# Scores of the first eight attention jobs as one plain f32 product from the loaded q and k, in two alternating operand sets

## The chip, the cores and the metric

The kernel runs on one core of one Trainium2 chip. The metric is device time in microseconds (us), the median of three runs. Five engines work side by side, each in its own order: TensorE (PE; its weight loads are shown apart as PEld), VectorE (DVE), ScalarE (ACT), GpSimd (POOL) and SyncE (SP), which here only issues DMA transfers. ACT issues some too.

## The reference

Causal attention with a distance bias, then a two-layer feed-forward network (FFN). Batch 8, 8 heads, 576 positions, head width 64; the FFN goes from 512 to 2048 and back. q and k are drawn eight times wider than `_attn_setup` says.

```python
scores = scale * np.matmul(q, k.transpose(0, 1, 3, 2))        # scale = 1/8
cum = np.cumsum(np.maximum(s, 0.0), axis=-1)
bias = -(cum[:, :, :, None] - cum[:, :, None, :])
scores = np.where(causal, -1000000000.0, scores + np.minimum(bias, 0.0))
attn = softmax(scores)            # max taken off, exp, sum + 1e-9
x = attn @ v                      # (4608, 512) over all heads
h = x @ w_in
g = np.where(h >= 1, h, np.where(h <= -1, 0.0, (h + 1) ** 2 / 4))
out = g @ w_out
```

## The kernel before, in words

**Jobs.** Attention is cut into 64 jobs: a pair of heads `n` (four pairs to a batch) and a half `hf` of the query positions. Half 0 has 320 queries (query tiles 0 to 2), half 1 has 256 (tiles 3 and 4). The list `jobs` goes batch by batch, first the four pairs of half 0, then the four of half 1; the first eight jobs are all of batch 0. A job has six score units (`UNITS`): a query tile of one head against the keys up to it, 64, 192, 320, 448 or twice 288 keys wide. So a job of half 0 has 2 x (64 + 192 + 320) = 1152 score columns, one of half 1 has 2 x 448 + 4 x 288 = 2048.

**Scores from split operands.** `att_load` (L307) fetches q and k of a job as f32 into `rq` and `rk`, each twice, to partitions 0 to 63 and again to 64 to 127 (four transfers on SP's queue, L316). `att_prep` (L320) makes four operands in a rounded format (F32R) of them:

- `Q1`: upper half the rounded -q/8 (ACT, L325), lower half what the rounding lost (DVE, L336)
- `K1`: the rounded k in both halves (ACT, L334)
- `Q2`: the rounded -q/8 again (ACT, L335), with four more rows for the bias
- `K2`: what rounding k lost (GpSimd for the first twelve jobs, L339), with four bias rows

The bias rows are the running sums of s, as a high and a low part, fetched by transfers on ACT's queue (L329 and L330 from SBUF for the first two jobs, L332 and L333 from DRAM for the others). Each score unit is then two products into one PSUM tile `s` (two buffers): L384 (`Q1` by `K1`, 128 rows deep) and L385 (`Q2` by `K2`, 68 rows deep). There is one set of `Q1`, `K1`, `Q2`, `K2`, so the next job's operands can be made only when the last score unit of the job before has been multiplied.

**After the scores.** DVE adds the mask and keeps the row minimum (L390; the scores carry a minus sign, so the minimum belongs to the greatest score); ACT takes the exponential (L401); `weights_t` scales the weights and splits them into two f16 parts on POOL, ACT and DVE (L422 to L428), and SP transposes them by DMA (L429). `att_out` multiplies by v (L447).

**Stages.** In the first, the loop over `NPAIR` jobs (L574) decodes the 16 pieces of w_in, which lie in memory as 64-bit numbers (ACT L192 and L199, DVE L193 to L203), four pieces per job, beside the four jobs of half 0. The buffers of the pieces are few, so a piece is fetched when an earlier one is decoded. Then `w1.scale` (L585) finds one scale over all pieces: DVE reduces, PE transposes (tile `row_wi`), DVE shortens (`top_wi`), PE spreads (`col_wi`), DVE inverts (`r_wi`). Only then are the pieces split into f16 pairs and the FFN can start; w_out's pieces are fetched only after that scale, too. In the second stage w_out is decoded and split in the same way, beside jobs 4 to 7 of half 1 and the FFN products of half 0 (L502 the first layer, L541 the second). From then on each step has attention and FFN in a fixed mix.

**What sets the order.** The program is written as one stream; a scheduler orders each engine's instructions ahead of time by its own estimate of times and by priorities given in the code (`high_priority`, `issue_after`). On the chip every engine follows its list strictly.

Of the kernel before, what the change touches and what calls it, by code (L numbers as in the profile page):

```python
# [9 lines left out]
F32 = mybir.dt.float32  # L10
F32R = mybir.dt.float32r
# [3 lines left out]
AF = mybir.ActivationFunctionType  # L15
ALU = mybir.AluOpType
# [6 lines left out]
P = 128  # L23
# [8 lines left out]
BIG = 1e9  # L32
# [27 lines left out]
K_POOL = range(12)  # L60
V_POOL = 4
# [3 lines left out]
FIRST_N = 1  # L65
# [8 lines left out]
def attention_ffn(ctx: ExitStack, tc: tile.TileContext, qT, kT, vT, s, w_in, w_out, yT):  # L74
    nc = tc.nc
    LOADQ, CUMQ, FIRSTQ = nc.sync, nc.scalar, nc.sync
# [35 lines left out]
    def spread(dst, top, name):  # L112
# [11 lines left out]
        fill=BIG, base=448, channel_multiplier=1,  # L124
# [181 lines left out]
    def att_load(n, hf):  # L306
# [3 lines left out]
        W = q0 + N  # L310
        rq = ap.tile([P, 2, N], F32, tag="rq", bufs=1, name=f"rq{n}_{hf}")
        rk = ap.tile([P, 2, W], F32, tag="rk", bufs=1, name=f"rk{n}_{hf}")
        for t, src, c0 in ((rq, qT, q0), (rk, kT, 0)):
            sv = src[b, h0:h0 + 2, :, c0:W].rearrange("h d n -> d h n")
            for d0 in (0, D):
                (FIRSTQ if jobs.index((n, hf)) < FIRST_N else LOADQ).dma_start(t[d0:d0 + D], sv)  # L316
        raws[n, hf] = rq, rk

    def att_prep(n, hf):

        rq, rk = raws.pop((n, hf))
# [3 lines left out]
        A.activation(Q1[:, :, :N], rq, AF.Copy, scale=-0.125)  # L325
        if jobs.index((n, hf)) < CH_N:
            for hd in range(2):
                r = ch[2 * n + hd:2 * n + hd + 1]
                CUMQ.dma_start(Q2[D:D + 2, hd, :N].bitcast(F32), r[:, :, q0:W].bitcast(F32))  # L329
                CUMQ.dma_start(K2[D + 2:D + 4, hd, :W].bitcast(F32), r[:, :, :W].bitcast(F32))  # L330
        else:
            CUMQ.dma_start(Q2[D:D + 2, :, :N].bitcast(F32), cd[:, :, q0:W])  # L332
            CUMQ.dma_start(K2[D + 2:D + 4, :, :W].bitcast(F32), cd[:, :, :W])  # L333
        A.copy(K1[:, :, :W], rk)  # L334
        A.activation(Q2[:D, :, :N], rq[:D], AF.Copy, scale=-0.125)  # L335
        V.scalar_tensor_tensor(  # L336
            Q1[D:, :, :N], rq[D:], -0.125, Q1[D:, :, :N].bitcast(F32), ALU.mult, ALU.subtract
# [33 lines left out]
    def scores(n, i, hd, c0, c1):  # L371
# [12 lines left out]
        T.matmul(sc[:R, :c1 - c0], Q1[:, hd, qo:qo + R], K1[:, hd, c0:c1], start=True, stop=False)  # L384
        T.matmul(sc[:R, :c1 - c0], Q2[:KC, hd, qo:qo + R], K2[:KC, hd, c0:c1], start=False, stop=True)  # L385
# [278 lines left out]
```

## Time and profile before

| What | Value |
|---|---|
| Median of 3 runs | 1128.73 us (1127.24 to 1128.74) |
| Span of the profiled execution (first to last instruction) | 1126.2 us |
| The profiled execution's own time | not on the page; the median is 2.5 us over the span |
| PE busy | 988.1 us, 88% |
| DVE busy | 876.6 us, 78% |
| ACT busy | 745.2 us, 66% |
| POOL busy | 693.1 us, 62% |
| PE busy from 232 to 262 us | 29.88 of 30.00 us |
| PE busy from 30 to 60 us | 9.20 of 30.00 us |
| `r_wi` (scale of w_in) written | 88.2 us |

The page gives one execution. Busy shares are over the whole span and hide that the first fifth of the program is limited by other engines than the rest; the view by windows shows it. A row of the timeline has the start, the duration, the engine, the line and operation, output and inputs, and in brackets how long the engine had been idle and what released it. Durations of PE overlap, since matmuls are pipelined.

### The profile page before, as it was taken

The numbers are of one execution on the slowest core, as the hardware profiler recorded it, in microseconds if no ns is written. First come the engines' busy times: TensorE is split into PE (matmuls) and PEld (weight loads), VectorE is DVE, ScalarE is ACT, GpSimd is POOL, SyncE is SP. The second block draws the span as 40 slices with busy tenths as digits, with TensorE's granted clock in tenths as the row PEclk, the third lists the DMA queues.
The fourth block names the chain that finished last, engine by engine and source line by source line (L and its number), as shares of the span: only waits on it lengthen the run. The fifth ranks groups of instructions, "written<-read, shape, count | busy, mean of one in ns | idle before, by whom it ended". The sixth has DMA issues, their size and how long they took to land.

```text
span 1126.2 us, 25201 instructions
## 1 busy us (share of the span) xinstructions
PE 988.1 (88%) x8470; PEld 771.8 (69%) x8470; DVE 876.6 (78%) x2396; ACT 745.2 (66%) x1727; POOL 693.1 (62%) x1177
## 2 busy tenths in 40 slices
PE   1233587799999999989999999999999999899998
PEld 0122355578777877778777877787778777787787
DVE  7999996778777887778778877888788877787533
ACT  4667687677747775767657774777577765777432
POOL 3867279776547764676647754776467664765522
PEclk9997987889999999999999999999999999999999
DMA  8995546677739774778647763877467864666300
GB/s 235 214 204 149 164 110 137 123 158 163 151 74 190 153 172 86 150 170 144 142 86 189 165 143 75 191 169 166 86 148 171 152 136 84 157 156 138 66 24 20
DMA packets 343082, 158.05 MB, mean 140 GB/s; under 512 B 291112, under 2 KB 324264, under 8 KB 342952
## 3 DMA queue, kind: packets, MB, share of 16 engines
q1 hardware_dynamic: 333248, 146.50, 60.7%
q10 hardware_dynamic: 9704, 9.93, 2.8%
q8 instruction: 67, 1.10, 0.4%
q14 instruction: 63, 0.52, 0.1%
HBM read 75.33 MB, written 9.73 MB: 76 GB/s over the span
## 4 chain that ended last, share of the span: by engine, by line
PE 48%; DVE 6%; POOL 5%; issue 3%; ACT 3%; DMA 2%; ACTq 0%; DVEq 0%; POOLq 0%
PE h L502 20%; PE y L541 20%; PE px L447 3%; PE s L384 3%; PE s L385 2%; DMA pt<-pb 2%; DVE pb L428 1%; DVE Q L336 1%; POOL g L529 1%; POOL pb L422 1%; ACT u L514 1%; ACT p L401 1%; POOL vb L350 1%; POOL pb L425 1%; DVE p L390 1%
## 5 line engine op out<-in xcount | busy, mean ns | idle before, releaser
L502 PE MATMUL h<-x,WI 128*128 128x256 f16 (+1 forms) x3072 | 464.7, 291 | 30.3 <-DVE u L518 24.7
L541 PE MATMUL y<-g,WO 128*128 128x256 f16 (+1 forms) x3072 | 456.7, 288 | 7.5 <-POOL g L529 5.3
L502 PEld LDWEIGHTS <-WI 128*128 128x128 f16 x3072 | 291.2, 99 | 124.0 <-issue 34.2
L541 PEld LDWEIGHTS <-WO 128*128 128x128 f16 x3072 | 287.3, 98 | 91.8 <-issue 12.5
L529 POOL TENSOR_TENSOR g<-u,g 128x320 f16<-128x320 f32 (+1 forms) x256 | 204.0, 797 | 162.1 <-ACT g L528 161.3
L401 ACT ACTIVATE p<-p,mn 64x64 f32<-64x64 f32 (+4 forms) x320 | 179.6, 561 | 134.9 <-DVE mn L390 113.1
L514 ACT ACTIVATE u<-h,ub,us 128x320 f32<-128x320 f32 (+1 forms) x256 | 149.3, 584 | 122.8 <-PE h L502 117.8
L517 DVE SCALAR_TENSOR_TENSOR h<-h,ws,u 128x320 f32<-128x320 f32 (+1 forms) x256 | 132.5, 518 | 103.8 <-ACT u L514 101.2
L422 POOL TENSOR_SCALAR pb<-p,rs 64x128 f16<-64x128 f32 (+4 forms) x160 | 97.3, 608 | 165.2 <-DVE rs L418 105.1
L384 PE MATMUL s<-K,Q 128*128 128x288 f32 (+4 forms) x384 | 149.2, 391 | 55.9 <-DVE mn L390 25.9
L425 POOL TENSOR_TENSOR pb<-p,pb 64x128 f16<-64x128 f32 (+4 forms) x160 | 172.8, 1080 | 9.2
L428 DVE SCALAR_TENSOR_TENSOR pb<-p,rs,pb 64x128 f16<-64x128 f32 (+4 forms) x160 | 143.1, 894 | 43.0 <-POOL pb L422 42.7
L390 DVE CUSTOM_DVE_ANT_0 p<-s,mask 64x64 f32<-64x64 f32 (+4 forms) x320 | 134.4, 421 | 27.5 <-PE s L385 24.2
L518 DVE SCALAR_TENSOR_TENSOR u<-u,r,h 128x320 f32<-128x320 f32 (+1 forms) x256 | 130.3, 509 | 6.3
L384 PEld LDWEIGHTS s<-K,Q 128*128 128x128 f32 (+1 forms) x384 | 73.7, 192 | 81.3 <-DVE mn L390 36.1
L385 PE MATMUL s<-K,Q 68*128 68x288 f32 (+4 forms) x384 | 122.3, 320 | 5.1 <-DMA K<-cumd 2.6
L423 ACT ACTIVATE p<-p,rs 64x64 f32<-64x64 f32 (+4 forms) x160 | 89.8, 561 | 55.1 <-DVE rs L418 54.1
L528 ACT CAST g<-u 128x320 f16<-128x320 f32 (+1 forms) x256 | 108.3, 423 | 9.6 <-DVE u L518 9.5
L447 PE MATMUL px<-pt,vt 128*64 128x256 f16 (+3 forms) x1536 | 82.4, 258 | 18.3 <-DMA pt<-pb 8.1
L424 POOL TENSOR_SCALAR pb<-p 64x128 f16<-64x128 f32 (+4 forms) x160 | 91.8, 574 | 10.7 <-ACT p L423 9.5
L447 PEld LDWEIGHTS <-vt 128*64 128x64 f16 x1536 | 73.1, 113 | 36.4 <-issue 28.3
L385 PEld LDWEIGHTS s<-K,Q 68*128 68x128 f32 (+1 forms) x384 | 75.0, 196 | 9.0 <-POOL K L339 3.2
(115 smaller groups left out, 961.4 us busy)
## 6 DMA issues: line engine op xcount, KB each, us to landing
rk<-in_k_dram SPq DMA_DIRECT2D x64, 288.0 KB
rq<-in_q_dram SPq DMA_DIRECT2D x64, 160.0 KB
rk<-in_k_dram SPq DMA_DIRECT2D x64, 160.0 KB
v<-in_v_dram SPq DMA_DIRECT2D x32, 288.0 KB
wir<-in_moe_w_in_dram SPq DMA_DIRECT2D x16, 512.0 KB
rq<-in_q_dram SPq DMA_DIRECT2D x64, 128.0 KB
wor<-in_moe_w_out_dram SPq DMA_DIRECT2D x16, 512.0 KB
out_dram<-o ACTq DMA_DIRECT2D x32, 160.0 KB
```

The lines of the kernel that those rows point to most:

```text
L384: T.matmul(sc[:R, :c1 - c0], Q1[:, hd, qo:qo + R], K1[:, hd, c0:c1], start=True, stop=False)
L385: T.matmul(sc[:R, :c1 - c0], Q2[:KC, hd, qo:qo + R], K2[:KC, hd, c0:c1], start=False, stop=True)
L390: ttr[0] = V.tensor_tensor_reduce(out=Pt[:R, c0:c1], in0=sc[:R, :c1 - c0], in1=mask[:R, mo:mo + c1 - c0], scale=1.0, scalar=3.0e38 if mn i ...
L401: A.activation(Pt[:R, :W], Pt[:R, :W], AF.Exp, bias=m2[:R], scale=-1.0, accum_out=sums[n, i][:R, hd:hd + 1])
L425: G.tensor_tensor(los[1], pw, his[1], ALU.subtract)
L428: V.scalar_tensor_tensor(los[0], pv, rs[:R, :1], his[0], ALU.mult, ALU.subtract)
L447: T.matmul(px[hd * D:(hd + 1) * D, lo:N], VT[:, vl * NB + j, hd * D:(hd + 1) * D], PT[:, 4 * j + 2 * hd + pl, lo:], start=(m == 0), stop=( ...
L502: T.matmul(h[:, :N], WI[4 * kt + ft // 4][:, wl, ft % 4 * P:(ft % 4 + 1) * P], x[:, kt, xl], start=(n == 0), stop=(n == 3 * NKT - 1),)
L514: first = A.activation(u, h[:, :N], AF.Relu, bias=ubi[b], scale=usc[b]).ins
L517: V.scalar_tensor_tensor(h[:, :N], h[:, :N], wsc[b], u, ALU.mult, ALU.max)
L529: G.tensor_tensor(g[:, 1], u, g[:, 0], ALU.subtract)
L541: T.matmul(ys[b, hf, m][:, :N], WO[8 * (m // 2) + ft // 2][:, wl, c0:c0 + P], g[:, gl], start=(ft == 0 and n == 0), stop=(ft == NFT - 1 an ...
```

## The change

For the first eight jobs the scores are one product per unit, of plain f32 operands as loaded. Two sets of operands, `QF[0]`, `KF[0]` and `QF[1]`, `KF[1]`, are used in turn. They lie in the buffers that `rq`/`rk` and `Q1`/`K1` have later. `att_load` writes q and k straight into partitions 0 to 63 of a set and the bias rows into the four below; so the bias transfers of a job are issued with its loads, one job ahead, and not in `att_prep`, which returns at once for these jobs. The constant bias rows are 8 and -8, and the factor 1/8 with its sign goes to the mask instruction (`scale=-0.125`). From job 8 on everything is done as before, with the sign moved in the same way (`scale=-1.0`).

```diff
...
@@ -121,17 +121,23 @@
     G.memset(mask, 0.0)
     G.affine_select(
         out=mask, in_=mask, pattern=[[-1, S]], compare_op=ALU.is_ge,
-        fill=BIG, base=448, channel_multiplier=1,
+        fill=-8.0 * BIG, base=448, channel_multiplier=1,
     )
 
     KC = D + 4
     NQ = HALF[0][1]
-    Q1 = cp.tile([P, 2, NQ], F32R, name="Q1")
-    K1 = cp.tile([P, 2, S], F32R, name="K1")
     Q2 = cp.tile([P, 2, NQ], F32R, name="Q2")
     K2 = cp.tile([P, 2, S], F32R, name="K2")
-    G.memset(Q2[D:KC].bitcast(F32), -1.0)
-    G.memset(K2[D:KC].bitcast(F32), 1.0)
+    G.memset(Q2[D:KC].bitcast(F32), 1.0)
+    G.memset(K2[D:KC].bitcast(F32), -1.0)
+
+    QF, KF = [], []
+    for i, (tq, tk) in enumerate((("rq", "rk"), ("q1", "k1"))):
+        QF.append(ap.tile([P, 2, NQ], F32, tag=tq, bufs=1, name=f"QF{i}"))
+        KF.append(ap.tile([P, 2, S], F32, tag=tk, bufs=1, name=f"KF{i}"))
+        G.memset(QF[i][D:KC], 8.0)
+        G.memset(KF[i][D:KC], -8.0)
+    one = []
 
 
     BH = B * H
@@ -308,33 +314,48 @@
         b, h0 = n // NPAIR, 2 * (n % NPAIR)
         q0, N, _ = HALF[hf]
         W = q0 + N
+        j = jobs.index((n, hf))
+        if j < F32_JOBS:
+            q, k = QF[j % 2], KF[j % 2]
+            for t, src, c0 in ((q[:D, :, :N], qT, q0), (k[:D, :, :W], kT, 0)):
+                LOADQ.dma_start(t, src[b, h0:h0 + 2, :, c0:W].rearrange("h d n -> d h n"))
+            cd = cumd[2 * n:2 * n + 2].rearrange("h l n -> l h n")
+            if j < CH_N:
+                for hd in range(2):
+                    r = ch[2 * n + hd:2 * n + hd + 1]
+                    CUMQ.dma_start(q[D:D + 2, hd, :N], r[:, :, q0:W].bitcast(F32))
+                    CUMQ.dma_start(k[D + 2:D + 4, hd, :W], r[:, :, :W].bitcast(F32))
+            else:
+                CUMQ.dma_start(q[D:D + 2, :, :N], cd[:, :, q0:W])
+                CUMQ.dma_start(k[D + 2:D + 4, :, :W], cd[:, :, :W])
+            return
         rq = ap.tile([P, 2, N], F32, tag="rq", bufs=1, name=f"rq{n}_{hf}")
         rk = ap.tile([P, 2, W], F32, tag="rk", bufs=1, name=f"rk{n}_{hf}")
         for t, src, c0 in ((rq, qT, q0), (rk, kT, 0)):
             sv = src[b, h0:h0 + 2, :, c0:W].rearrange("h d n -> d h n")
             for d0 in (0, D):
-                (FIRSTQ if jobs.index((n, hf)) < FIRST_N else LOADQ).dma_start(t[d0:d0 + D], sv)
+                LOADQ.dma_start(t[d0:d0 + D], sv)
         raws[n, hf] = rq, rk
 
     def att_prep(n, hf):
 
+        if jobs.index((n, hf)) < F32_JOBS:
+            return
+        if not one:
+            one.append(ap.tile([P, 2, NQ], F32R, tag="q1", bufs=1, name="Q1"))
+            one.append(ap.tile([P, 2, S], F32R, tag="k1", bufs=1, name="K1"))
+        Q1, K1 = one
         rq, rk = raws.pop((n, hf))
         q0, N, _ = HALF[hf]
         W = q0 + N
         cd = cumd[2 * n:2 * n + 2].rearrange("h l n -> l h n")
-        A.activation(Q1[:, :, :N], rq, AF.Copy, scale=-0.125)
-        if jobs.index((n, hf)) < CH_N:
-            for hd in range(2):
-                r = ch[2 * n + hd:2 * n + hd + 1]
-                CUMQ.dma_start(Q2[D:D + 2, hd, :N].bitcast(F32), r[:, :, q0:W].bitcast(F32))
-                CUMQ.dma_start(K2[D + 2:D + 4, hd, :W].bitcast(F32), r[:, :, :W].bitcast(F32))
-        else:
-            CUMQ.dma_start(Q2[D:D + 2, :, :N].bitcast(F32), cd[:, :, q0:W])
-            CUMQ.dma_start(K2[D + 2:D + 4, :, :W].bitcast(F32), cd[:, :, :W])
+        A.activation(Q1[:, :, :N], rq, AF.Copy, scale=0.125)
+        CUMQ.dma_start(Q2[D:D + 2, :, :N].bitcast(F32), cd[:, :, q0:W])
+        CUMQ.dma_start(K2[D + 2:D + 4, :, :W].bitcast(F32), cd[:, :, :W])
         A.copy(K1[:, :, :W], rk)
-        A.activation(Q2[:D, :, :N], rq[:D], AF.Copy, scale=-0.125)
+        A.activation(Q2[:D, :, :N], rq[:D], AF.Copy, scale=0.125)
         V.scalar_tensor_tensor(
-            Q1[D:, :, :N], rq[D:], -0.125, Q1[D:, :, :N].bitcast(F32), ALU.mult, ALU.subtract
+            Q1[D:, :, :N], rq[D:], 0.125, Q1[D:, :, :N].bitcast(F32), ALU.mult, ALU.subtract
         )
         (G if jobs.index((n, hf)) in K_POOL else V).tensor_tensor(
             K2[:D, :, :W], rk[:D], K1[:D, :, :W].bitcast(F32), ALU.subtract
@@ -381,15 +402,22 @@
             G.memset(Pt[:R, W:W + D], 0.0)
         Pt = pbs[n, i][hd]
         sc = ps_s.tile([P, 512], F32, tag="s", name=f"s{n}_{i}_{hd}_{c0}")
-        T.matmul(sc[:R, :c1 - c0], Q1[:, hd, qo:qo + R], K1[:, hd, c0:c1], start=True, stop=False)
-        T.matmul(sc[:R, :c1 - c0], Q2[:KC, hd, qo:qo + R], K2[:KC, hd, c0:c1], start=False, stop=True)
+        j = jobs.index((n, i // 3))
+        if j < F32_JOBS:
+            T.matmul(
+                sc[:R, :c1 - c0], QF[j % 2][:KC, hd, qo:qo + R], KF[j % 2][:KC, hd, c0:c1], start=True, stop=True
+            )
+        else:
+            Q1, K1 = one
+            T.matmul(sc[:R, :c1 - c0], Q1[:, hd, qo:qo + R], K1[:, hd, c0:c1], start=True, stop=False)
+            T.matmul(sc[:R, :c1 - c0], Q2[:KC, hd, qo:qo + R], K2[:KC, hd, c0:c1], start=False, stop=True)
         mn = mins.pop((n, i, hd), None)
         m2 = ap.tile([P, 1], F32, tag="mn", bufs=6, name=f"mn{n}_{i}_{hd}_{c0}")
         mo = 448 - off + c0
         with tc.high_priority(offset=TTR_LEAD):
             ttr[0] = V.tensor_tensor_reduce(
                 out=Pt[:R, c0:c1], in0=sc[:R, :c1 - c0], in1=mask[:R, mo:mo + c1 - c0],
-                scale=1.0, scalar=3.0e38 if mn is None else mn[:R],
+                scale=-0.125 if j < F32_JOBS else -1.0, scalar=3.0e38 if mn is None else mn[:R],
                 op0=ALU.add, op1=ALU.min, accum_out=m2[:R],
             ).ins
         if late:
```

The scheduler sees other instructions and so makes other lists, but only in the first fifth of the program: from the first second-layer products of half 1 (L541, about 232 us in the profile of before) PE's list is the same to the end, and on the other engines too the lists run alike from within the next few jobs of batch 1.

At the start of ACT's list (the bias transfers and the operands of job 0, between the first pieces of w_in; `wir` is a raw piece of w_in, `WO` the buffer that it is decoded into). Before:

```order
L192 ACTIVATE WO1_125<-wir1_152 128x512
L329 DMA Q2_91<-ch_103 2x1x320
L330 DMA K2_92<-ch_103 2x1x320
L325 ACTIVATE Q1_89<-rq0_0_156 128x640
L329 DMA Q2_91<-ch_103 2x1x320
L330 DMA K2_92<-ch_103 2x1x320
L334 CAST K1_90<-rk0_0_157 128x2x320
L335 ACTIVATE Q2_91<-rq0_0_156 64x640
L192 ACTIVATE WO2_126<-wir2_154 128x512
```

After:

```order
L198 ACTIVATE WO_131<-wir_158 128x512
L326 DMA QF_93<-ch 2x1x320
L327 DMA KF_94<-ch 2x1x320
L326 DMA QF_93<-ch 2x1x320
L327 DMA KF_94<-ch 2x1x320
L326 DMA QF_97<-ch 2x1x320
L327 DMA KF_98<-ch 2x1x320
L326 DMA QF_97<-ch 2x1x320
L327 DMA KF_98<-ch 2x1x320
L429 ACTIVATE p_0_0_206,sm_0_205<-p_0_0_206,mn_0_0_0_210 64x64
L198 ACTIVATE WO_132<-wir_160 128x512
```

The three operand instructions are gone, and the bias transfers of job 1 (set 97 and 98) stand with those of job 0.

On DVE where the scale of the second half of w_out is found (`row_wo1` is PE's transposed maxima, `pb1_3` the f16 weights of pair 1, query tile 3; `Q1` an operand of job 6). Before:

```order
L518 SCALAR_TENSOR_TENSOR u0_0_15_1610<-u0_0_15_1610,r0_797,h0_0_15_1597 128x320
L336 SCALAR_TENSOR_TENSOR Q1_89<-rq2_1_1285,Q1_89 64x2x256
L428 SCALAR_TENSOR_TENSOR pb1_3_1277<-p1_3_0_1224,rs1_3_1278,pb1_3_1277 128x4x128
L109 TENSOR_REDUCE top_wo1_1459<-row_wo1_1457 1x1
L211 TENSOR_SCALAR top_wo1_1459<-top_wo1_1459 1x1
```

After:

```order
L546 SCALAR_TENSOR_TENSOR u0_0_15_1513<-u0_0_15_1513,r0_741,h0_0_15_1500 128x320
L445 TENSOR_SCALAR rs1_4_1328<-sm1_4_1242 128x2
L446 RECIPROCAL rs1_4_1328<-rs1_4_1328 128x2
L109 TENSOR_REDUCE top_wo1_1373<-row_wo1_1371 1x1
L217 TENSOR_SCALAR top_wo1_1373<-top_wo1_1373 1x1
```

The operand of job 6 is gone from ahead of the scale, and the weights `pb1_3`, which stood right ahead of the reduction, now stand 14 rows ahead of it.

On PE right behind that, at the first scores of job 6 (`col_wo1` spreads the scale; `h0_1` and `y0_0` are FFN products). Before:

```order
L117 MATMUL col_wo1_1467<-t16_wo1_1465,ones_82 128x1
L384 MATMUL s2_3_0_0_1560<-K1_90,Q1_89 128x448
L385 MATMUL s2_3_0_0_1560<-K2_92,Q2_91 128x448
L384 MATMUL s2_3_1_0_1570<-K1_90,Q1_89 128x448
L385 MATMUL s2_3_1_0_1570<-K2_92,Q2_91 128x448
L502 LDWEIGHTS WI0_108
L502 MATMUL h0_1_0_2174<-x0_1_1452,WI0_108 128x256
```

After:

```order
L117 MATMUL col_wo1_1381<-t16_wo1_1379,ones_82 128x1
L407 MATMUL s2_3_0_0_1467<-KF0_94,QF0_93 128x448
L530 LDWEIGHTS WI0_114
L530 MATMUL h0_1_0_2062<-x0_1_1366,WI0_114 128x256
L530 LDWEIGHTS WI0_114
L530 MATMUL h0_1_1_2094<-x0_1_1366,WI0_114 128x256
```

One product per unit stands where two stood, and FFN products come between the units.

More of the change, by code (lines that the diff above doesn't have):

```diff
@@ L60 @@
 K_POOL = range(12)
+F32_JOBS = 8
 V_POOL = 4
@@ L64 @@
 W2_RATE = 2
-FIRST_N = 1
 CH_N = 2
@@ L75, in attention_ffn @@
     nc = tc.nc
-    LOADQ, CUMQ, FIRSTQ = nc.sync, nc.scalar, nc.sync
+    LOADQ, CUMQ = nc.sync, nc.scalar
     V, A, G, T = nc.vector, nc.scalar, nc.gpsimd, nc.tensor
```

## The prediction

> **What bounds the kernel now.** I read the page's slices first, then the view by windows, then the timelines of PE, DVE and POOL up to 232 us.
>
> ```profile
> span 1126.2 us, 25201 instructions
> ...
> PE   1233587799999999989999999999999999899998
> ...
> DVE  7999996778777887778778877888788877787533
> ...
> PEclk9997987889999999999999999999999999999999
> DMA  8995546677739774778647763877467864666300
> ```
>
> One digit is 28 us. From the ninth slice PE is busy all the time at the full clock; before that it is not, DVE is, and in the first three slices so are the DMA engines. The windows put numbers on it (columns: stretch, its length, then busy time and count for PE, PEld, DVE, ACT, POOL, then granted clock, DMA share and GB/s).
>
> ```profile
> 0.00:30.00 30.00, 3.45 (x12) 2.18 (x12) 21.98 (x56) 14.87 (x25) 11.75 (x26) 1.00 0.82 231
> 30.00:60.00 30.00, 9.20 (x42) 6.78 (x42) 27.35 (x74) 18.91 (x40) 22.27 (x36) 1.00 0.95 218
> 60.00:88.00 28.00, 8.54 (x53) 6.26 (x52) 25.08 (x67) 15.46 (x40) 21.03 (x37) 1.00 0.90 199
> ...
> 144.00:172.00 28.00, 20.00 (x143) 13.49 (x141) 27.62 (x61) 23.39 (x45) 21.19 (x20) 0.93 0.37 89
> 172.00:202.00 30.00, 26.30 (x159) 17.21 (x158) 20.26 (x43) 22.49 (x42) 27.47 (x32) 0.78 0.64 136
> 202.00:232.00 30.00, 21.42 (x161) 16.38 (x162) 21.36 (x78) 19.43 (x48) 22.46 (x38) 0.73 0.69 137
> 232.00:262.00 30.00, 29.88 (x295) 25.32 (x294) 23.15 (x69) 21.30 (x59) 23.50 (x47) 0.99 0.78 163
> ```
>
> The eight jobs lie before 211 us. From 232 us PE has no slack (29.88 of 30.00) and its list is the same in both kernels. So whatever the first 232 us lose or gain shifts everything behind it: the end moves by that amount. Two stages count. **Stage A**, up to 88.2 us, when the scale of w_in is written: DVE is 90% busy from 30 us on (27.35 + 25.08 of 58), the DMA engines 90 to 95%, PE a third. **Stage B**, 88 to 232 us: DVE is full until 172 (27.62 of 28), then POOL (27.47 of 30) and PE (26.30) share the limit.
>
> **Stage A, what goes.** The operands of jobs 0 to 4 are made there.
>
> ```profile
> L336 DVE SCALAR_TENSOR_TENSOR Q<-rq,Q 64x640 fp32r<-64x640 f32 x4 | 4.7, 1170 | 0.1
> L336 DVE SCALAR_TENSOR_TENSOR Q<-rq,Q 64x512 fp32r<-64x512 f32 x1 | 0.7, 689 | 0.0
> L339 POOL TENSOR_TENSOR K<-rk,K 64x640 fp32r<-64x640 f32 x4 | 6.8, 1705 | 10.0 <-DMA Q<-ch 9.5 <-ACT K L334 0.5
> ```
>
> DVE loses 4.7 + 0.7 = 5.4 us of work. It also loses waiting that is booked as work: while POOL runs L339, DVE instructions with two inputs take several times their usual length.
>
> ```profile
> 82.95 3.03 DVE L428 SCALAR_TENSOR_TENSOR pb<-p,rs,pb 128x384 f16<-128x384 f32 x1 [0.79 <-POOL pb L422]
> ...
> 82.96 2.60 POOL L339 TENSOR_TENSOR K<-rk,K 64x1152 fp32r<-64x1152 f32 x1
> ...
> 56.56 0.60 DVE L428 SCALAR_TENSOR_TENSOR pb<-p,rs,pb 128x384 f16<-128x384 f32 x1
> ...
> 50.96 1.91 DVE L203 SCALAR_TENSOR_TENSOR WO<-wir,WO 128x512 int32<-128x512 int32 x1
> ...
> 50.21 2.11 POOL L339 TENSOR_TENSOR K<-rk,K 64x640 fp32r<-64x640 f32 x1
> ...
> L203 DVE SCALAR_TENSOR_TENSOR WO<-wir,WO x8: 672/774/1914, 11.6 to 75.3; 128x512 int32<-128x512 int32 x8
> ```
>
> The same L428 takes 0.60 us alone and 3.03 beside L339: 2.4 us. The longest L203 (1914 ns against a least of 672) stands beside another L339: 1.2 us. Together 5.4 + 2.4 + 1.2 = 9.0 us of DVE. The gaps ahead of a job's first scores also go, since nothing has to be prepared:
>
> ```profile
> 35.34 0.29 PE L384 MATMUL s<-K,Q 128*64 128x64 f32 x1 [4.30 <-DVE Q L336]
> ...
> 52.75 0.29 PE L385 MATMUL s<-K,Q 68*64 68x64 f32 x1 [1.39 <-DMA K<-cumd]
> ```
>
> I give these gaps no price of their own, because DVE fills them with decoding. The transfers shrink as well:
>
> ```profile
> DMA packets 22470, 19.44 MB, mean 216 GB/s; under 512 B 16148, under 2 KB 18744, under 8 KB 22464
> ...
> rq<-in_q_dram SPq DMA_DIRECT2D x8, 160.0 KB
> rk<-in_k_dram SPq DMA_DIRECT2D x8, 160.0 KB
> rk<-in_k_dram SPq DMA_DIRECT2D x4, 288.0 KB
> rq<-in_q_dram SPq DMA_DIRECT2D x4, 128.0 KB
> ```
>
> These are the first 90 us: q and k are 16 x 160 + 4 x 288 + 4 x 128 = 4224 KB, half of it second copies. 2112 KB at 216 GB/s are 10.0 us of transfer. SP issues 12 transfers fewer (two of four per job, six jobs in that stretch). The bias transfers are not fewer; they move from the operands to the loads, a job earlier on ACT's queue, ahead of L198's later pieces, and wait only for `ch` or `cumd`.
>
> Stage A is held by a loop of fetching, decoding and attention in which DVE and DMA are both near full and both get about 10 us lighter. The upper bound is therefore 9 to 10 us. The lower bound is what stands on the last link: L428 at 82.95 and the L336 of 0.7 us stand on DVE right ahead of the reduction that gives the scale, 2.4 + 0.7 = 3.1 us. I take two thirds of DVE's 9.0: **6 us** (DVE is the busier of the two for the decoding, but a third of its relief will turn into waits for pieces).
>
> **Stage B, what goes.** Operands of jobs 5 to 7.
>
> ```profile
> 149.14 3.00 DVE L336 SCALAR_TENSOR_TENSOR Q<-rq,Q 64x512 fp32r<-64x512 f32 x1
> ...
> 167.15 0.69 DVE L336 SCALAR_TENSOR_TENSOR Q<-rq,Q 64x512 fp32r<-64x512 f32 x1
> 167.87 3.00 DVE L428 SCALAR_TENSOR_TENSOR pb<-p,rs,pb 128x512 f16<-128x512 f32 x1
> ...
> 185.48 2.49 DVE L417 TENSOR_SCALAR rs<-sm 128x2 f32<-128x2 f32 x1
> ...
> 172.00 0.16 PE L117 MATMUL col_wo<-t_wo,ones 1*128 1x1 bf16 x1 [2.59 <-DVE t_wo L115]
> ...
> 191.28 0.38 PE L502 MATMUL h<-x,WI 128*128 128x256 f16 x2 [2.46 <-ACT x L458]
> ...
> 184.94 3.00 POOL L339 TENSOR_TENSOR K<-rk,K 64x1152 fp32r<-64x1152 f32 x1
> ```
>
> At 149 us DVE is the limit: 3.0 us. At 167 us an L336 and a slow L428 stand ahead of the scale of w_out; in the new list neither does, and PE's idle 2.6 us behind them go. At 185 us L417, two columns wide, waits out an L339 (both end at 187.9); ACT's weights, its L458 and then PE wait for it, idle 2.5 us. Sum 3.0 + 2.6 + 2.5 = 8.1 us. POOL, near full there, gets two L339 lighter.
>
> **What is added: PE.** No row shows a plain f32 product of real data. One pass per column of a product:
>
> ```profile
> 178.35 3.42 PE L541 MATMUL y<-g,WO 128*128 128x320 f16 x12
> ...
> 181.90 3.43 PE L541 MATMUL y<-g,WO 128*128 128x320 f16 x24
> ...
> L384 PE MATMUL s<-K,Q 128*128 128x288 f32 x128 | 52.0, 406 | 0.1
> L385 PE MATMUL s<-K,Q 68*128 68x288 f32 x128 | 39.0, 304 | 0.0
> L385 PEld LDWEIGHTS s<-K,Q 68*128 68x128 f32 x320 | 65.7, 206 | 1.5 <-issue 0.6
> ```
>
> A product 320 columns wide takes 143 ns at the full clock (3.43 us for 24) and 285 ns at half (3.42 for 12): 0.45 and 0.89 ns a column. A job of half 1 has 2048 score columns and now takes two passes over them, L384 and L385. Bounds for the plain product: one pass below, which would save one; above, the four products of two high and two low parts, each at the mean of L385 and its weight load with nothing overlapped, 4 x (304 + 206) = 2040 ns for 288 columns where 406 + 304 = 710 ns stand now, 1.33 us more per unit. I take four passes, pipelined: the split operands cover three partial products in two passes by stacking two of them over 128 rows, and a product only 68 rows deep that keeps the same digits has at least those three and cannot stack them. So two passes more: 2 x 2048 x 0.45 = 1.84 us a job at the full clock, 2.4 at the granted 0.78. Jobs 0 to 4 pay it in PE's idle time (9.20 of 30 us busy), job 5 as well (20.00 of 28). Jobs 6 and 7 fall where PE itself is near the limit: 4.7 us. If job 5's cover were gone, 2.0 us more.
>
> [...]
>
> DVE's L390 has the same form with another factor and I cost it at nothing. The two sets of constant rows are four more memsets on POOL in the first 15 us, where it idles 9.5 us (the L339 row's wait).
>
> **Sum.** Stage A 6, stage B 8.1 - 4.7 = 3.4: 9.4 us off the span of 1126.2, so 1116.8. The median stands 2.5 us over that span, so **1119.3 us**. With A from 3.1 to 10 and B from 1.4 (job 5 uncovered) to 6, the likeliest case covers 1113 to 1124.
>
> **Rivals.**
>
> *PE becomes the bound (slower).* In stage B, 18 score units of jobs 5 to 7 cost 1.33 us more each, 24 us. PE idles 20.3 us of 144 to 232 (88 less 20.00, 26.30 and 21.42), of which half at most is usable, since the other half are waits for weights that stay. 24 - 10 - 6 from stage A: 8 us slower, **1137**. It decides from 16 / 18 = 0.9 us more per unit; four pipelined passes cost 0.3 (full clock) to 0.6 (half). For it: nothing in the rows has this operation. Against it: even at half the clock the passes reach two thirds of that.
>
> [...]
>
> *Both stages in full.* A brings 10 us, as DVE and DMA shrink alike, and B its 8.1, with PE's passes hidden by a clock that recovers sooner (0.78 and 0.73 in the windows): 18 us, **1111**. For it: the gaps of 4.30 and 1.39 us per job, which I left out. Against it: POOL at 27.47 of 30.
>
> *No gain.* The new list brings a transfer of v for batch 1 (288 KB, 1.4 us at 216 GB/s) forward among the pieces of w_in, and ACT's list has four bias transfers ahead of its third piece. If these and other moves of the list eat what is saved, **1128**. That the change does not do what it says is not a case: the lists show one product per unit and no operands for eight jobs.
>
> **How the numbers follow.** Forecast 0.53; pieces of w_in 0.18; both in full 0.11; PE the bound 0.10; no gain 0.08. What a measurement of this kernel can tell from no change is 0.2%, 2.3 us: 1126.5 to 1131.0. Faster: the forecast, both in full and two thirds of the pieces' case, 0.76. Same: the rest of that case and most of "no gain", 0.12. Slower: PE the bound and what is left of "no gain", 0.12. The range runs from the full case to no gain, **1111 to 1129**, and leaves out PE as the bound and the far side of both ends.
>
> **What would show it.** Right: `r_wi` written about 82 us instead of 88.2; L418 on DVE waiting no longer for PE than L390 did; the idle 2.59 and 2.46 us of PE gone; the first L569 of half 1 about 9 us before 232; the rest unchanged. The product's price: a 288-column unit near 0.7 us at most. Wrong: `r_wi` at 85 us or later (pieces of w_in, to be seen as ACT's waits for them); or PE at 29 of 30 us from 172 to 232 and units of 1.5 us or more.

## The result, and the profile after

The changed kernel takes 1112.13 us (median of 4 runs, 1110.62 to 1116.48) against 1128.74 us (4 runs, 1127.24 to 1131.14) before: a ratio of 0.9845, 95% interval 0.9821 to 0.9869. That is 16.6 us less, where 9.4 were forecast. The likeliest case had been given 1113 to 1124 us; the time lies just below that, inside the stated range of 1111 to 1129. The nearest case was the rival in which both stages bring all they have (1111 us). The page's slices of the changed kernel:

```profile
span 1109.9 us, 25106 instructions
...
PE   1355779699999999999999999999999999999998
...
PEclk9997999699999999999999999999999999999999
```

And its windows, columns as in the prediction:

```profile
30.00:60.00 30.00, 14.30 (x57) 8.34 (x59) 29.59 (x84) 17.71 (x44) 20.15 (x40) 1.00 0.91 217
60.00:88.00 28.00, 13.29 (x80) 8.25 (x76) 24.05 (x77) 17.11 (x38) 16.05 (x30) 1.00 0.76 202
...
172.00:202.00 30.00, 24.75 (x189) 17.12 (x186) 20.21 (x66) 18.80 (x41) 20.46 (x27) 0.90 0.55 125
202.00:232.00 30.00, 23.94 (x196) 19.21 (x196) 21.81 (x66) 19.38 (x55) 22.52 (x48) 0.76 0.82 162
232.00:262.00 30.00, 30.00 (x296) 25.74 (x296) 25.56 (x71) 23.60 (x59) 21.02 (x42) 1.00 0.80 161
```

From 232 us nothing is different in kind: PE is full. Ahead of it PE is busier in every stretch shown but the one from 172 us (26.30 to 24.75), DVE is fuller from 30 to 60 us (27.35 to 29.59 of 30) and a little less full from 60 to 88, and the DMA share has fallen (0.95 to 0.91, 0.90 to 0.76). Where the time went is read best from where the two stages join. First the timeline of before (DVE and PE; the first row is the first score of job 3, `t_wi` is the greatest value over the decoded pieces of w_in, `row_wi` its transpose on PE, `r_wi` the end of stage A, `r_wo` the scale of the second half of w_out; the last row is the first second-layer product of half 1):

```profile
69.80 0.28 PE L384 MATMUL s<-K,Q 128*64 128x64 f32 x1 [0.61 <-DVE mn L390]
...
73.05 0.15 DVE L208 TENSOR_REDUCE t_wi<-peak_wi 128x1 f32<-128x16 f32 x1
...
81.70 0.37 PE L107 MATMUL row_wi<-ident,t_wi 128*1 128x128 f32 x1
...
85.91 0.27 DVE L109 TENSOR_REDUCE top_wi<-row_wi 1x1 f32<-1x128 f32 x1
...
87.85 0.16 DVE L215 RECIPROCAL r_wi<-bound_wi 128x1 f32<-128x1 f32 x1
...
172.39 0.16 DVE L215 RECIPROCAL r_wo<-bound_wo 128x1 f32<-128x1 f32 x1
...
231.84 1.56 PE L541 MATMUL y<-g,WO 128*128 128x256 f16 x8
```

The same rows of the changed kernel, with the product of job 2's weights by v on PE:

```profile
63.06 0.47 PE L407 MATMUL s<-KF,QF 68*64 68x64 f32 x2 [2.67 <-DVE mn L418]
...
68.69 0.15 DVE L214 TENSOR_REDUCE t_wi<-peak_wi 128x1 f32<-128x16 f32 x1
...
71.91 1.66 PE L475 MATMUL px<-pt,vt 128*64 128x320 f16 x18 [0.23 <-DVE mn L418]
73.49 0.37 PE L107 MATMUL row_wi<-ident,t_wi 128*1 128x128 f32 x1
...
76.86 0.27 DVE L109 TENSOR_REDUCE top_wi<-row_wi 1x1 f32<-1x128 f32 x1
...
78.79 0.16 DVE L221 RECIPROCAL r_wi<-bound_wi 128x1 f32<-128x1 f32 x1
...
160.75 0.16 DVE L221 RECIPROCAL r_wo<-bound_wo 128x1 f32<-128x1 f32 x1
...
217.12 1.93 PE L569 MATMUL y<-g,WO 128*128 128x256 f16 x8
```

| Place | Before | After | Earlier by |
|---|---|---|---|
| first score of job 3 | 69.80 | 63.06 | 6.7 |
| last piece of w_in decoded (`t_wi`) | 73.05 | 68.69 | 4.4 |
| scale of w_in (`r_wi`) | 87.85 | 78.79 | 9.1 |
| second scale of w_out (`r_wo`) | 172.39 | 160.75 | 11.6 |
| first y of half 1 | 231.84 | 217.12 | 14.7 |
| span | 1126.2 | 1109.9 | 16.3 |

Stage A gave 9.1 us (6 forecast), stage B 14.7 - 9.1 = 5.6 (3.4 forecast), 2.6 of it by the second scale of w_out, and 1.6 more came in behind. The table also shows what I had overlooked: already in the kernel before, the decoding is done 12.9 us before `top_wi`. What ends stage A is not the decoding. `row_wi` stands on PE behind the product by v of an attention job, and `top_wi` on DVE behind that job's weights; both wait for the attention, not for the pieces. No run puts these small instructions ahead of the attention in the kernel before, which would show what their place in the lists alone costs.

The granted clock is a rival in stage B. It was 0.83 from 88 to 232 us before and 0.86 from 79 to 217 us after, so 24.5 and 19.3 us of full clock were missing. If PE were the bound all the way, the difference of 5.2 us would be nearly all of stage B's gain; PE is busy two thirds of the time there, and the runs do not tell how much of it counts. The gain as a whole is not the clock's: in the runs with a mean clock of 0.977 to 0.981 over the program, the kernel before took 1125.9 us and more, the changed one 1110.6 to 1116.5.

How PE waited for the attention in the first 90 us stands in its groups by line. Before:

```profile
L384 PE MATMUL s<-K,Q 128*64 128x64 f32 (+2 forms) x24 | 10.9, 462 | 41.4 <-DVE mn L390 20.4 <-ACT K L334 14.5 <-DVE Q L336 5.2
L385 PE MATMUL s<-K,Q 68*64 68x64 f32 (+2 forms) x24 | 9.3, 394 | 3.7 <-DMA K<-cumd 1.4 <-POOL K L339 1.2 <-DMA K<-ch 1.1
```

After:

```profile
L407 PE MATMUL s<-KF,QF 68*64 68x64 f32 (+3 forms) x52 | 22.9, 569 | 41.5 <-DVE mn L418 21.9 <-DMA cumd<-ch 16.2 <-DMA KF<-ch 1.5
```

The first score of each kernel on PE's timeline, before and then after:

```profile
14.49 0.42 PE L384 MATMUL s<-K,Q 128*64 128x64 f32 x2 [14.49 <-ACT K L334]
```

```profile
16.19 0.44 PE L407 MATMUL s<-KF,QF 68*64 68x64 f32 x2 [16.19 <-DMA cumd<-ch]
```

So the 14.5 us put down to ACT's operand are the start of the program, and in the changed kernel, where they are put down to the bias rows, they are 1.7 us longer. What is gone is the 5.2 us of waiting for DVE's operand and most of the 3.7 us ahead of L385. The waits for the two score buffers that DVE has to free are as long as before (20.4 and 21.9). In sum PE's idle time ahead of scores falls only from 45.1 to 41.5 us. The lead comes job by job: 1.7 us behind the old kernel at the first score, 6.7 ahead at the first score of job 3, 9.1 at the scale. How it is shared among the links of a job is not shown.

### The profile page after: what moved, and what is told of

Its sections match the earlier page's. It is cut to its first block, busy times and chain, and to the rows that moved or that the text cites. A ratio compares the mean times of both kernels' runs of the same rounds, so it can differ in the third digit from the quotient of the medians.

```text
span 1109.9 us, 25106 instructions
## 1 busy us (share of the span) xinstructions
PE 995.8 (90%) x8470; PEld 771.3 (69%) x8470; DVE 860.1 (77%) x2388; ACT 727.7 (66%) x1703; POOL 674.1 (61%) x1173
## 4 chain that ended last, share of the span: by engine, by line
PE 57%; DVE 11%; POOL 8%; DMA 6%; issue 6%; ACT 6%; SPq 0%; DVEq 0%; ACTq 0%; POOLq 0%
PE h L530 24%; PE y L569 23%; PE px L475 4%; PE s L412 3%; DMA pt<-pb 3%; PE s L413 3%; DMA wor<-in_moe_w_out_dram 2%; DVE pb L456 2%; ACT u L542 2%; POOL pb L450 2%; POOL pb L453 2%; ACT p L429 1%; DVE p L418 1%; POOL g L557 1%; DVE h L545 1%
## 5 line engine op out<-in xcount | busy, mean ns | idle before, releaser
L456 DVE SCALAR_TENSOR_TENSOR pb<-p,rs,pb 64x128 f16<-64x128 f32 (+4 forms) x160 | 135.1, 844 | 41.6 <-POOL pb L450 41.1
L412 PE MATMUL s<-K,Q 128*64 128x64 f32 (+1 forms) x336 | 126.2, 377 | 11.4 <-DVE mn L418 7.4
L413 PE MATMUL s<-K,Q 68*64 68x64 f32 (+1 forms) x336 | 103.0, 308 | 2.6 <-DMA K<-cumd 2.6
L407 PE MATMUL s<-KF,QF 68*128 68x288 f32 (+4 forms) x96 | 40.6, 536 | 43.4 <-DVE mn L418 22.1
L412 PEld LDWEIGHTS s<-K,Q 128*64 128x64 f32 (+1 forms) x336 | 61.4, 183 | 22.8 <-DVE mn L418 7.7
```

What stands on the lines that cost most here:

```text
L456: V.scalar_tensor_tensor(los[0], pv, rs[:R, :1], his[0], ALU.mult, ALU.subtract)
```

## The experiments

Gains below are (1 - ratio) x 1128.7 us, each ratio against the kernel before on the same chip, so that runs on different chips can be compared. The changed kernel gains 17.5 us by that measure (16.6 by the medians above).

### How many jobs: 4, 16, 12

```diff
-F32_JOBS = 8
+F32_JOBS = 4
```

> Plain product for jobs 0 to 3 only; jobs 4 to 7 prepare split operands as before. Against 1112.1 us with eight jobs and 1128.7 us with none. If the gain is the sum of two stages (9.0 us by the scale of w_in, 5.7 us from there to 224 us, as the two profiles show), stage A keeps its 9.0 less the last link (job 4's operand on DVE beside job 4's L339 right ahead of the reduction, about 3 us): 1122 to 1123 us. If only an early start of the whole chain counts and stage B merely inherits it: 1114 to 1116 us.

1122.1 us, ratio 0.9930 (0.9910 to 0.9951): 7.9 us of gain. `r_wi` is at 80.20, so four jobs bring 7.6 of the 9.1 us of stage A; jobs 4 to 7 bring the other 9.6 us of the gain. The time is that of the first theory, but not from where it was expected: the scale lost 1.4 us and not 3, and the first y (225.34) is only 6.5 us ahead of the kernel before, so stage B got 1.1 us longer.

```diff
-F32_JOBS = 8
+F32_JOBS = 16
```

> Plain product for jobs 0 to 15. Jobs 10 to 15 lie where PE was 100% busy. If PE is the limit there, each pays two more passes: 4 x 1.04 us for half 0 and 4 x 1.84 us for half 1 at the full clock, 11.5 us together, less 2 to 3 us for jobs 8 and 9 whose place still has idle PE time: 1120 to 1122 us. If preparation stalls PE there as much as the passes cost: 1110 to 1113 us.

1121.76 us, ratio 0.9918 (0.9886 to 0.9950): 9.3 us of gain, 8.2 less than with eight jobs. The eight further jobs fall where PE is full. This run's groups on PE from 232 to 340 us, at the full clock, give the price of the product (a unit is booked as two instructions):

```profile
L530 PE MATMUL h<-x,WI 128*128 128x320 f16 x192 | 30.8, 299 | 0.3 <-DVE u L546 0.3
...
L530 PE MATMUL h<-x,WI 128*128 128x256 f16 x132 | 17.6, 273 | 0.0
...
L407 PE MATMUL s<-KF,QF 68*128 68x288 f32 x32 | 10.5, 409 | 0.0
L407 PE MATMUL s<-KF,QF 68*128 68x448 f32 x16 | 7.3, 539 | 0.0
```

An f16 product 64 columns wider takes 26 ns longer: 0.41 ns a column. An f32 unit 160 columns wider takes 2 x (539 - 409) = 260 ns longer: 1.63 ns a column, four times as much. So it is four passes of the f16 kind. The two split products take about one each: in the kernel before, from 262 to 1000 us at the full clock, L384 goes from 342 ns at 192 columns to 452 at 448 and L385 from 277 to 413, 0.43 and 0.53 ns a column. Two passes more than the split pair, over 4 x 1152 + 4 x 2048 columns, are 2 x 12800 x 0.41 = 10.5 us. Where PE is by then is seen from ACT's first work on a job's product by v. Jobs 12 and 31 of the changed kernel:

```profile
277.39 0.46 ACT L486 ACTIVATE x<-px,ex 128x256 f16<-128x256 f32 x1
...
577.02 0.45 ACT L486 ACTIVATE x<-px,ex 128x256 f16<-128x256 f32 x1
```

The same with sixteen jobs:

```profile
275.20 0.48 ACT L486 ACTIVATE x<-px,ex 128x256 f16<-128x256 f32 x1
...
584.32 0.45 ACT L486 ACTIVATE x<-px,ex 128x256 f16<-128x256 f32 x1
```

Job 12 (275.20) is still 2.2 us ahead of the changed kernel (277.39), job 31 is 7.3 behind it. These 9.5 us lie between the two passes of jobs 12 to 15 alone (6.7 us) and those of all eight jobs (10.5).

```diff
-F32_JOBS = 8
+F32_JOBS = 12
```

> Plain product for jobs 0 to 11. With sixteen, the offset to before was best between jobs 10 and 12 (about 2 us better than with eight) and was lost from job 13 on. If the four jobs of half 0 in batch 1 gain where PE still has idle time and the half-1 jobs cost: 1110 to 1111 us. If PE's two more passes cost there as well: 4 x 1.04 us more, 1115 to 1116 us.

1113.29 us, ratio 0.9859 (0.9831 to 0.9887), not to be told from eight, and between the two answers foreseen.

### One set of operands

```diff
-            q, k = QF[j % 2], KF[j % 2]
+            q, k = QF[0], KF[0]
```

and the same in the product. Nothing else of the change is undone.

> As the change, but one set of operands, so a job's loads wait until the last score of the job before. If the gain is work taken off DVE and POOL, DVE fills the gaps with decoding: 1113 to 1116 us. If it is the chain from load to scores that got shorter, each of seven jobs waits about 3 us for its loads again, and three of them in stage A count: 1120 to 1125 us.

1129.74 us, ratio 0.9988 (0.9964 to 1.0011): the whole gain is gone, more than either theory had allowed. PE now waits for each job's k, which cannot be fetched before the last score of the job ahead. The kernel before did not have that wait: `rq` and `rk` took the loads early (job 2's k is issued from 36.94 us, while job 1's last score starts at 46.11). PE and DVE on its timeline:

```profile
45.99 4.01 PE L407 MATMUL s<-KF,QF 68*128 68x192 f32 x8 [8.35 <-DMA KF<-in_k_dram]
...
60.97 0.16 DVE L214 TENSOR_REDUCE t_wi<-peak_wi 128x1 f32<-128x16 f32 x1
...
63.50 4.05 PE L407 MATMUL s<-KF,QF 68*128 68x192 f32 x8 [8.42 <-DMA KF<-in_k_dram]
...
84.56 0.16 DVE L221 RECIPROCAL r_wi<-bound_wi 128x1 f32<-128x1 f32 x1
```

This run shows most plainly what bounds stage A. With attention stalled, the decoding is done at 60.97, 7.7 us earlier than in the changed kernel, and `r_wi` is still 5.8 us later. It does not show what the removed work is worth by itself: this kernel has all of it removed, but it has also lost the early loads that the kernel before had. It shows that loading straight into the operands needs the second set.

### Putting back one piece of work at a time

Each of these kernels adds, for the eight jobs, work as large as what the change removed. Nothing reads its result.

The second copies of q and k, to the upper partitions (60 of 64 rows, as the four bias rows lie there now):

```diff
+            for t, src, c0 in ((q[KC:, :, :N], qT, q0), (k[KC:, :, :W], kT, 0)):
+                LOADQ.dma_start(t, src[b, h0:h0 + 2, :P - KC, c0:W].rearrange("h d n -> d h n"))
```

> As the change, but the second copies of q and k are fetched again, 60 of the 64 rows each, to partitions 68 to 127, where nothing reads them: 94% of the bytes that the change removed, and its transfers. If the transfers limited stage A, up to 10 us come back: 1117 to 1122 us. [...]

1116.48 us, ratio 0.9874 (0.9842 to 0.9906): 3.3 us lost, though the two intervals overlap, and just under the 1117 to 1122 us foreseen for transfers as the limit. Its window shows the DMA share at 1.00, and the scale comes 2.6 us later:

```profile
30.00:60.00 30.00, 11.12 (x40) 6.88 (x40) 27.23 (x79) 18.08 (x41) 20.38 (x36) 1.00 1.00 241
...
81.40 0.16 DVE L221 RECIPROCAL r_wi<-bound_wi 128x1 f32<-128x1 f32 x1
```

DVE's operand:

```diff
+            V.scalar_tensor_tensor(
+                Q2[:D, :, :N], q[:D, :, :N], 0.125, q[:D, :, :N], ALU.mult, ALU.subtract
+            )
             return
```

> As the change, but DVE makes a lower part of q for each of the eight jobs as before (same shape, nothing waits for it until job 8). If DVE's work limits stage A and B, its 8 x 0.7 to 0.8 us come back in full, 5 to 6 us: 1117 to 1118 us. If the chain from load to scores is what was shortened, 1 to 2 us: 1113 to 1114 us.

1119.27 us, ratio 0.9909 (0.9889 to 0.9928): 7.2 us lost, 3.7 of them by `r_wi` (82.46). That is more than the first theory allowed, and the trace shows why it is not DVE's work alone. The group over the whole program, then DVE's timeline at the scale of w_in:

```profile
L347 DVE SCALAR_TENSOR_TENSOR Q<-QF 64x640 fp32r<-64x640 f32 (+1 forms) x8 | 6.3, 787 | 9.4 <-DMA QF<-in_q_dram 9.3
```

```profile
79.01 0.71 DVE L347 SCALAR_TENSOR_TENSOR Q<-QF 64x512 fp32r<-64x512 f32 x1 [2.71 <-DMA QF<-in_q_dram]
```

The eight instructions take 6.3 us, and DVE idles 9.3 us more until their q has landed. The one at 79.01 stands in DVE's list between `top_wi` (76.03, 0.8 us earlier than in the changed kernel) and the instructions that finish the scale; its wait of 2.71 us, its own 0.71 and the weights right behind it (1.25 us) are the delay.

POOL's operand:

```diff
+            G.tensor_tensor(K2[:D, :, :W], k[:D, :, :W], k[:D, :, :W], ALU.subtract)
             return
```

> As the change, but POOL subtracts k from k for each of the eight jobs, with the shape that its operand had before, into a buffer that nothing reads until job 8; no score waits for it. If POOL's own time and the DVE instructions that it slows are a main part of the gain, 5 to 8 us come back: 1117 to 1120 us. If the gain is the chain from load to scores, 0 to 2 us: 1112 to 1114 us.

1126.88 us, ratio 0.9981 (0.9963 to 0.9999): 15.4 us lost, nearly the whole gain, for eight instructions. Both theories missed this by 6.9 us and more.

All of them at once, with ACT's three as well:

```diff
+            A.activation(Q2[:D, :, :N], q[:D, :, :N], AF.Copy, scale=0.125)
+            A.copy(K2[:D, :, :W], k[:D, :, :W])
+            A.activation(Q2[:D, :, :N], q[:D, :, :N], AF.Copy, scale=0.125)
```

> As the change, with all removed work put back beside it (second copies, three ACT, one DVE and one POOL instruction per job), but no score waits for any of it. If removed work is the gain, it is as slow as before: 1126 to 1129 us. If half of the gain is that scores no longer wait for the preparation, 1119 to 1122 us. If only the waiting counts, 1114 to 1116 us.

1137.55 us, ratio 1.0066 (1.0048 to 1.0084): slower than before, and 24.9 us lost. The losses one at a time, 3.3 + 7.2 + 15.4 = 25.9 us, come to nearly the same, although ACT's three instructions were in none of them. So the pieces do add up, to 7.4 us more than the change gained. Either the product by itself is dearer than the pair by up to that much, or the work stands worse here than it did before: its instructions wait for the loads in each engine's order and for each other (POOL's eight idle 7.2 us until ACT has written the same tile). No run separates the two.

### Why POOL's eight instructions cost 15 us

The subtraction from the loaded k does three things: it takes POOL's time, it makes POOL wait for k to land, and it reads SBUF beside DVE. Its group over the whole program, then POOL's timeline around that of job 3 (L455 and L457 make the weights of job 1's last tile):

```profile
L347 POOL TENSOR_TENSOR K<-KF 64x640 fp32r<-64x640 f32 (+1 forms) x8 | 15.5, 1934 | 10.2 <-DMA KF<-in_k_dram 10.2
```

```profile
53.51 0.59 POOL L455 TENSOR_SCALAR pb<-p,rs 128x384 f16<-128x384 f32 x1 [1.79 <-DVE rs L451]
55.18 2.96 POOL L347 TENSOR_TENSOR K<-KF 64x640 fp32r<-64x640 f32 x1 [1.08 <-DMA KF<-in_k_dram]
58.12 1.89 POOL L457 TENSOR_SCALAR pb<-p 128x384 f16<-128x384 f32 x1
```

Between the first and the second step of the weights stand 1.08 us of waiting and 2.96 of work for a later job. That the reading holds the set is not the matter here: it ends at 58.14, and the next load into that set, for job 5, is issued at 79.42. Two runs put the same work back without the wait:

```diff
+            for hd in range(2):
+                G.tensor_tensor(K2[:D, hd, :W], mask[:D, :W], mask[:D, :W], ALU.subtract)
             return
```

> The changed kernel; POOL makes, for each of the eight jobs and at the same place of its order, a subtraction as large as the one removed (L339), but from the mask and into the idle K2: it waits for no transfer and holds no operand set. Nothing reads the result. Three theories for why one subtraction per job on POOL gave back 14.8 us when it read the loaded k. (a) The set is held: POOL waits for k in its own order, so the weights behind it and the next load come later; then this kernel loses only a little, 1113 to 1117. (b) POOL reading SBUF stretches DVE's two-input work: 1121 to 1127. (c) POOL's own 15.5 us: 1121 to 1127 as well, told from (b) by the memset run.

```diff
+            for _ in range(1 + hf):
+                G.memset(K2[:D, :, :W].bitcast(F32), 0.0)
+            G.memset(Q2[:D, :, :N].bitcast(F32), 0.0)
             return
```

> The changed kernel; at the same place POOL makes memsets of the lower parts of Q2 and K2, by the row of a 4x1152 memset (1.207 us) about 15.5 us in all for the eight jobs, as long as the eight subtractions together. They read nothing, wait for no transfer and hold no operand set; nothing reads them. (a) held set: 1112 to 1116. (b) DVE stretched beside a POOL that reads: 1112 to 1116, and clearly below the run with the mask. (c) POOL's own time: 1121 to 1127, as the run with the mask.

1116.12 us (0.9887, 0.9869 to 0.9905) and 1115.12 us (0.9890, 0.9871 to 0.9910): about 5 us lost by each. By what was written beforehand, that would have settled it for the wait. It did not, because the two kernels differ from the one with the loaded k in more than the wait. With nothing to wait for, the scheduler put the work where POOL had been idle:

```profile
8.85 9.59 POOL L346 TENSOR_TENSOR K<-mask 64x320 fp32r<-64x320 f32 x10
```

All of it was done by about 36 us. What the two runs tell is that whether POOL reads or only writes made no difference to the time there (at the scale of w_in they are 3.9 and 1.0 us late). So the last run ties the same subtractions to their places, behind the clearing of the job's first score buffers on POOL:

```diff
-            G.memset(Pt[:R, W:W + D], 0.0)
+            ms = G.memset(Pt[:R, W:W + D], 0.0)
+            if hd and i in (0, 3) and jobs.index((n, i // 3)) < F32_JOBS:
+                w = sum(HALF[i // 3][:2])
+                with tc.issue_after(ms.ins):
+                    for x in range(2):
+                        G.tensor_tensor(K2[:D, x, :w], mask[:D, :w], mask[:D, :w], ALU.subtract)
```

> The changed kernel with the mask subtractions of the run before (as large as L339, nothing reads them), but each pair tied behind the clearing of its job's first score buffers on POOL. In POOL's list they now stand where the run with the loaded k had its subtraction, ahead of or between the weights of the job before, and no longer in the first 36 us. They still wait for no transfer and hold no operand set. Two theories for the 14.8 us that subtraction gave back. Place: about 2 us of POOL per job stand on the way from the scores to the weights, the transpose and the next stage, whatever they read: 1121 to 1127, with r_wi written at about 85 us. Wait: what counted is POOL standing idle (10.2 us in all) until k had landed: 1114 to 1117, with r_wi at 81 us or earlier.

1125.17 us (10 runs, 1118.75 to 1129.90), ratio 0.9949 (0.9927 to 0.9971): 11.7 us lost. POOL and DVE, and PE's first y of half 1:

```profile
50.58 1.44 POOL L407 TENSOR_TENSOR K<-mask 64x320 fp32r<-64x320 f32 x2
...
80.68 0.16 DVE L221 RECIPROCAL r_wi<-bound_wi 128x1 f32<-128x1 f32 x1
...
226.99 2.22 PE L574 MATMUL y<-g,WO 128*128 128x256 f16 x12
```

| Later than in the changed kernel by | `r_wi` | first y of half 1 | gain lost |
|---|---|---|---|
| subtraction of the loaded k | 6.8 | 16.0 | 15.4 |
| subtraction of the mask, in its place | 1.9 | 9.9 | 11.7 |
| subtraction of the mask, early | 3.9 | 0.6 | 4.7 |

The time answers "place", the row that I had tied to it answers "wait". In stage A the wait for k matters (6.8 us of delay with it, 1.9 without). In stage B both runs lose alike (6.8 to 16.0 is 9.2 more, 1.9 to 9.9 is 8.0 more), which speaks for the place. By the first y the same work costs 0.6 us when it is done early and 9.9 between the weights. The clock keeps this from being settled. From 81 to 227 us the tied run was granted 0.79, the changed kernel 0.86 from 79 to 217: 11.4 us of full clock more were missing, so all of the 8.0 us could be the clock's. With the loaded k (0.84 from 86 to 233) it is 4.2 us more, so there at least 5.0 of the 9.2 us are not. Behind the first y, with lists that soon are the same, the tied run's profile loses 5.0 us more and that of the early one 2.2. In the tied run the clock was lower in three stretches (0.86, 0.91 and 0.93 from 330 to 350, 480 to 500 and 835 to 860 us, against 0.91, 1.00 and 1.00), an estimated 4.6 us where PE is full.

### Less for POOL elsewhere

If POOL's share in the chain counts, taking the low part of v off it should bring more:

```diff
-V_POOL = 4
+V_POOL = 0
```

> The changed kernel with the low part of v made on DVE for every pair (V_POOL = 0 where it was 4): POOL loses eight instructions of 128x576 in the first stages (3.2 + 5.1 us), DVE gains four of one input pair. If POOL's time or POOL beside DVE is what the change had relieved, more relief brings more: 1106 to 1110. If what counted was the waiting of POOL for the loads, nothing is left there and DVE, the fuller engine, gets heavier: 1112 to 1116.

1111.75 us, ratio 0.9849 (0.9833 to 0.9865): the time of the changed kernel, between the two answers foreseen. The decoding is done at 61.95 (6.7 us earlier), and `r_wi` comes only 2.2 us earlier (76.59). The profiled execution, the fastest of its four, keeps these 2 us to the end (span 1107.4); the median does not show them. No version beat the changed kernel beyond the noise.

## Why the prediction was right, and what in it was wrong

**That the first 232 us decide** held: of 16.3 us in the span 14.7 are there at the first y of half 1, and PE is full behind it (30.00 of 30).

**Stage A, 6 us forecast, 9.1 measured.** The scale, put at 88.2 us before and about 82 after, was written at 79.2. The step that failed is the one on the gaps ahead of a job's first scores: "I give these gaps no price of their own, because DVE fills them with decoding". DVE does fill them, but the decoding is not what is waited for. `t_wi` at 73.05 in the kernel before, 12.9 us ahead of `top_wi`, said so in the very trace I read, and the run with one set shows it (decoding done at 60.97, scale at 84.56). So the "loop of fetching, decoding and attention in which DVE and DMA are both near full" was the wrong picture: much of DVE's fullness is decoding that is done too early to matter. What holds the scale is the chain of each job from its operands over scores, weights and transposes to the product by v, and the waits of 4.30 and 1.39 us stand in it. The upper bound of 9 to 10 us came out about right for another reason, which is luck.

**DVE beside POOL** was sized at 2.4 + 1.2 us from two rows, one of the weights and one of the decoding. The groups from 0 to 88 us show more for the first and nothing for the second. Before:

```profile
L203 DVE SCALAR_TENSOR_TENSOR WO<-wir,WO 128x512 int32<-128x512 int32 x8 | 8.3, 1036 | 0.1
...
L428 DVE SCALAR_TENSOR_TENSOR pb<-p,rs,pb 128x384 f16<-128x384 f32 x4 | 5.3, 1333 | 3.8 <-POOL pb L422 3.8
```

After (L209 is L203's counterpart, L456 that of L428):

```profile
L209 DVE SCALAR_TENSOR_TENSOR WO<-wir,WO 128x512 int32<-128x512 int32 x8 | 10.0, 1251 | 0.0
...
L456 DVE SCALAR_TENSOR_TENSOR pb<-p,rs,pb 128x384 f16<-128x384 f32 x4 | 3.3, 826 | 2.1 <-POOL pb L450 2.1
```

The widest weights alone give 5.3 - 3.3 = 2.0 us back, the 256 wide ones another 1.8 (934 ns to 492 ns, four each). The decoding was not relieved: the eight L209 took 10.0 us where the eight L203 took 8.3, so the term of 1.2 us did not come. DVE's busy time from 0 to 88 us rose from 74.4 to 76.2 us; 9.0 less had been worked out, though the last 9 us of that stretch are stage B in the changed kernel.

**Stage B, 3.4 us forecast, 5.6 measured.** The sum came near by two errors that offset each other. By the second scale of w_out the prediction has 3.0 + 2.6 = 5.6 us, and 2.6 were measured; behind it 2.5 - 4.7 = -2.2, and 3.1 were measured. Two of the three waits named there are gone. The second scale of w_out finds no slow weights ahead of it any more, and PE no longer idles 2.59 us there (the last row is the wait spoken of below):

```profile
149.57 0.15 DVE L214 TENSOR_REDUCE t_wo<-peak_wo 128x1 f32<-128x8 f32 x1
...
158.70 0.27 PE L107 MATMUL row_wo<-ident,t_wo 128*1 128x128 f32 x1
...
160.35 0.17 PE L117 MATMUL col_wo<-t_wo,ones 1*128 1x1 bf16 x1
...
206.04 2.77 PE L475 MATMUL px<-pt,vt 128*64 128x256 f16 x30 [3.24 <-DMA pt<-pb]
```

The decoding has been done for 9.1 us when `row_wo` starts, as with `row_wi`; here 24 second-layer products (3.43 us from 155.11) stand ahead of it on PE. The third wait, 2.46 us of PE, was replaced by another: PE idles 3.24 us at 206.04, for transposed weights. The 4.7 us charged for PE's passes in jobs 6 and 7 were too much: PE is busy 24.75 and 23.94 of 30 us there, so part of them can be hidden, and the higher clock from 172 us (0.90, 0.78 before) can hide some too; no run parts the two. Where PE really is full, the passes cost what was worked out (9.5 us seen, 6.7 to 10.5 worked out).

**The product's price** was right. Four passes were my estimate, with no row of a plain f32 product behind it; the run with sixteen jobs shows 1.63 ns a column against 0.41 for f16, and a 288-column unit takes 0.65 us (at 149.70 us), where near 0.7 at most was given as the sign.

**The rivals.** PE as the bound fell with that price. That the pieces of w_in hold stage A (0.18 in the chances) was my supposition, and the runs show otherwise: they are decoded long before its end (`t_wi` at 73.05 and `r_wi` at 87.85 before, 68.69 and 78.79 after), and putting the second copies back cost only 3.3 us. "Both in full" came nearest, but not by its own sum: stage A brought 9.1 of its 10 us, stage B 5.6 of its 8.1, and 1.6 came in behind the first y, so that 1111 lay so near is in part luck. Both of the reasons named for it are seen: the gaps of 4.30 and 1.39 us are gone, and the clock is higher (0.90 and 0.76 in the last two windows ahead of 232 us, 0.78 and 0.73 before).

**Not foreseen at all:** that the loads a job ahead, which the second set allows, are a condition of the whole gain (one set: 0.9988), and that POOL's L339 weighed most of all pieces. I had put it down for what it does to DVE; when put back, its wait for k and, as far as the clock lets one tell, its place between the weights of the job before cost more.

## What to carry to other kernels

Where two streams meet (here decoding and attention ahead of a scale), look up when each is ready before pricing anything: the busier one is not always the later one. Work that prepares the next job on an engine with a strict order costs what it delays behind it, and its wait for a transfer as well, which can be several times its duration (2.71 us for an instruction of 0.71). A removal test therefore has to keep the waits apart from the work. Loading straight into the operands gives up the early load that a staging buffer allowed; a second set gives it back (ratio 0.9988 with one set, 0.9845 with two). And a wait in a profile that is put down to an operand can be the start of the program: look at when it lies.

## What the runs showed of the hardware

A plain f32 product is booked as two instructions a unit and takes 1.63 ns a column at the full clock, against 0.41 for f16 (the run with sixteen jobs, 232 to 340 us). The eight subtractions on POOL took 15.5 us with the loaded k, 16.0 from the mask in about the same places. With the second copies fetched again the DMA share from 30 to 60 us was 1.00 instead of 0.91, and the scale of w_in came 2.6 us later; the memset run, which fetches none, has 1.00 there as well and a scale 1.0 us later, so the share by itself does not explain the delay.
